# A planner's entry for four small products is changed from 110 to 225 each

## The chip, the cores and the metric

The kernel runs on one core of a Trainium2 chip. The metric is the device time of one execution in microseconds (us). Before the change it is 2021.24 us, the median of three runs (2019.19 to 2022.35). The profile that is quoted here comes from one execution of its own, which took 2021.44 us.

A core has five engines that run side by side, each in the order of its own program: PE (TensorE; its weight loads are listed apart, as PEld), DVE (VectorE), ACT (ScalarE), POOL (GpSimd) and SP (SyncE, which here issues most of the DMAs). PE writes its results to PSUM, which has eight banks.

## The reference

```python
x = A_x                                           # 2048 x 512, fp32
mod = (silu(c) @ w_mod).reshape(1, 6, 1, -1)
sa, ca, ga, sb, cb, gb = (mod[:, i] for i in range(6))
h = layernorm(x) * (1 + ca) + sa
x = x + ga * attention(h, A_wqkv, A_wo)           # 32 heads of 16, softmax over 2048 keys
h = layernorm(x) * (1 + cb) + sb
x = x + gb * mixer(h, B_w1, B_w2, B_w3, B_w4)     # shifts along the sequence, then an MLP of 1792
```

The attention is the long part: for each of 32 heads, 2048 x 2048 scores, their exponentials, and the product with V.

## The kernel before

**Stages.** A prologue makes the layer norm, the modulation rows and the first columns of Q, K and V. The attention follows, from about 100 to 1535 us of the span. The rest of Q, K and V is made between the products of the first units of the attention. A tail (the product with `wo`, the mixer, the MLP) ends the kernel.

**Units.** The attention runs over 64 units: 4 chunks of 512 queries, times 16 pairs of heads. A unit has 16 key tiles of 128 keys, and each key tile has two half rows, one for each head of the pair, so a unit has 32 half rows. For a half row, PE makes two products side by side on different rows of its array: `sc` (L1012), 512 scores of the present unit, and `mb` (L996), scores of a unit that is 24 key tiles ahead, from which only the maximum is wanted. DVE reduces `mb` to a maximum (`mx`, L992). ACT takes the exponential of `sc` (`pt`, L1008) into integers of 32 bits. Their upper halves are read as fp16 as they stand. The lower halves have to be converted first, one instruction for each key tile: the function `p_low` gives it to POOL (L1061), or to ACT when the planner's clock for POOL is more than 200 ahead of that for ACT (the profile lists those under L156, the planner's line that calls them). PE then adds up P V from the upper halves (`pv`, L1086) and the lower halves (L1083) in one PSUM bank that stays with the unit.

**Blocks.** PE's program is made of blocks: three half rows (six products into six different banks of the seven that go round), then the `pv` products that are due. A unit is 10 and two thirds blocks, so that the pattern repeats after three units and 32 blocks. Units are numbered from 0; unit u is of the first, second or third kind as u divided by 3 leaves 0, 1 or 2.

**The shift rows.** When all maxima of a unit are there, `max_fin` makes its row of shifts: a reduction on DVE (L1042), two small copies on ACT (L1043, L1044), a difference on POOL (L1045), and then eight small DMAs issued by SP (`qtl<-nm`), which write the shifts as extra rows into the Q tile `qtl`. The first `sc` product of that unit reads these rows.

**The end of a unit.** ACT copies the finished sums to SBUF (`ac`, L1103). The first `pv` product of the next unit overwrites the same bank and has to wait for that copy. Then `o_fin` (L1107) transposes the sums with four products, `ot` (L1113), into one of the seven banks. ACT copies the result out (`sm`, L1120), which frees that bank; DVE takes the reciprocals of the row sums (`rc`, L1128), and POOL writes the quotients (L1124).

**The planner.** No engine chooses an order on the chip. When the kernel is built, a class `Sched` keeps a clock for each engine. `put` (L154) adds the cost of an instruction to its engine's clock and emits it; everything is emitted in the order that these clocks give. Work like `o_fin` is a generator: after each product it yields its cost, and `one` (L213) takes that from a budget and adds it to PE's clock. `fill` (L234) runs generators at the end of a block, as far as the budget goes. `gap` (L203) runs them when PE's clock would have to wait 500 or more for a bank or for `pt`, until the wait is filled up to 60. PE's clock also sets when a chain of the other engines counts as ready, when `p_low` prefers ACT, and when a bank counts as free.

Of the kernel before, what the change touches and what calls it, by code (L numbers as in the profile page):

```python
# [330 lines left out]
def kernel(ctx, tc, A_x, A_wqkv, A_wo, B_w1, B_w2, B_w3, B_w4, c, w_mod, out):  # L331
# [23 lines left out]
    def mark(key):  # L355
        return None, 0, lambda: done.add(key)
# [68 lines left out]
    def dbank(n):  # L425
        return sch.take(lambda i: psd["d"].tile([P, CH], F32, name=n, tag=f"s{i}" if psd["s"] else f"d{i}", bufs=1))
# [669 lines left out]
    def ac_copy():  # L1096
        u, e = acs.pop()
        while u and ("ot", u - 1) not in done:
            sch.step()
        ac = at.tile([P, CH], F32, name="ac", tag="ac", bufs=1)  # L1100
        vst.pop(u)
        acc = pv.pop(u)
        e = sch.crit("A", cA(), e + PX, lambda: act.activation(ac, acc, AF.Copy))  # L1103
        v_free[0] = e + XP["A"]
        sch.add(o_fin(u, ac, e + XP["A"]), 0)

    def o_fin(u, ac, ready):  # L1107
        ci, pr = units[u]
        yield lambda: sch.T["P"] >= ready and sch.room()
        n = 2 * (DH + 1)  # L1110
        b = dbank("ot")[:, :TPC * n]
        for t in range(TPC):
            te.matmul(b[:, t * n:(t + 1) * n], ac[:, t * P:(t + 1) * P], smat.rearrange("p j d -> p (j d)"), start=True, stop=True)  # L1113
            yield 110
        done.add(("ot", u))
        sm = at.tile([P, 8, DH + 1], F32, name="sm", tag="sm", bufs=2)
        rc = at.tile([P, 8, 1], F32, name="rc", tag="rc", bufs=2)

        def sums():
            act.activation(sm.rearrange("p th d -> p (th d)"), b, AF.Copy)  # L1120
            sch.free(b)

        def fin():
            pool.tensor_tensor(osb[ci][:, :, pr * 32:pr * 32 + 32].rearrange("p t (h d) -> p t h d", d=DH),  # L1124
                              sm[:, :, 0:DH].rearrange("p (t h) d -> p t h d", h=2),
                              rc.rearrange("p (t h) o -> p t h o", h=2).to_broadcast([P, TPC, 2, DH]), op=OP.mult)

        sch.chain(("A", 170, sums), ("D", 90, lambda: dve.reciprocal(rc, sm[:, :, DH:DH + 1])), ("G", 350, fin),  # L1128
                  *([mark(("att", ci))] if pr == NP - 1 else []), prio=0, bank=b)
# [601 lines left out]
```

## Time and profile before

| | us |
|---|---|
| median of three runs | 2021.24 |
| the profiled execution | 2021.44 |
| its span, first to last instruction | 2019.7 |
| PE busy in the span | 1934.4 (96%) |
| DVE busy | 1656.3 (82%) |
| POOL busy | 1571.9 (78%) |
| ACT busy | 1510.2 (75%) |

The profiled execution lies 0.2 us above the median, and 1.7 us of it lie outside the span. From about 500 to 1490 us the attention runs with nothing between its products but the four products of each unit: there all four engines are above 90%.

### The profile page before, as it was taken

How to read it: one execution, taken by the hardware profiler on the slowest of the kernel's cores; microseconds unless marked ns; L12 is line 12 of the kernel's file. 1: busy time of each engine (PE TensorE's matmuls, PEld its weight loads, DVE VectorE, ACT ScalarE, POOL GpSimd, SP SyncE). 2: the span in 40 equal slices, each digit the busy share in tenths (PEclk: the TensorE clock that was granted, in tenths of full speed). 3: DMA queues.
4: the chain of work that ended last, by engine and by line, in shares of the span. 5: the costliest groups of instructions: out<-in, count | busy, mean ns of one | idle time of the engine just before them, and what ended most of it. 6: DMA issues, size and time to landing. Idle time of an engine off the chain costs nothing.

```text
span 2019.7 us, 41655 instructions
## 1 busy us (share of the span) xinstructions
PE 1934.4 (96%) x14456; PEld 1162.1 (58%) x14456; DVE 1656.3 (82%) x2979; ACT 1510.2 (75%) x3085; POOL 1571.9 (78%) x1488
## 2 busy tenths in 40 slices
PE   7999999999999999999999999999998999999999
PEld 5755545454444444444444444444455878898998
DVE  6398888879999999999999999999975886556443
ACT  6438987768999999999999999999985544344443
POOL 6349988879999999999999999999996554435222
PEclk9989999999999999999999999999999999999999
DMA  8777675445343434444443435354414676553541
GB/s 295 233 204 192 151 187 155 135 130 124 86 92 87 91 88 83 96 82 97 81 98 75 104 72 107 72 136 126 99 46 158 230 261 265 226 200 116 201 153 68
DMA packets 185508, 278.01 MB, mean 138 GB/s; under 512 B 117104, under 2 KB 127856, under 8 KB 169008
## 3 DMA queue, kind: packets, MB, share of 16 engines
q1 hardware_dynamic: 181792, 267.20, 49.1%
q10 hardware_dynamic: 2304, 4.20, 0.6%
q0 software_dynamic: 1200, 3.93, 0.5%
q8 instruction: 115, 1.88, 0.4%
q14 instruction: 97, 0.79, 0.1%
HBM read 211.81 MB, written 62.91 MB: 136 GB/s over the span
## 4 chain that ended last, share of the span: by engine, by line
PE 61%; DVE 16%; ACT 9%; issue 6%; POOL 4%; DMA 3%; SPq 0%; ACTq 0%; POOLq 0%; DVEq 0%
PE mb L996 13%; DVE mx L992 12%; PE pv L1086 9%; PE sc L1012 8%; ACT pt L1008 7%; PE w L363 5%; PE w L359 5%; PE w L361 5%; PE pv L1083 4%; PE ot L1113 3%; POOL pt L1061 2%; PE xT L1247 1%; POOL trs L1356 1%; PE v L359 1%; DMA wr<-Ws 1%
## 5 line engine op out<-in xcount | busy, mean ns | idle before, releaser
L1061 POOL TENSOR_SCALAR pt<-pt 128x1024 f16<-128x1024 uint16 x953 | 1248.3, 1367 | 79.9 <-ACT pt L1008 76.7
L992 DVE TENSOR_REDUCE mx<-mb 128x1 f32<-128x512 f32 x2048 | 1250.0, 681 | 72.7 <-PE mb L996 63.5
L1008 ACT ACTIVATE pt<-sc 128x512 int32<-128x512 f32 x2048 | 1060.9, 614 | 123.5 <-PE mb L996 97.1
L996 PE MATMUL mb<-kst,qtl 62*128 62x512 f32 x2048 | 781.1, 461 | 20.5 <-ACT pt L1008 10.0
L1012 PE MATMUL sc<-qtl,kst 64*128 64x512 f32 x2048 | 739.3, 449 | 4.6 <-DVE mx L992 1.8
L996 PEld LDWEIGHTS mb<-kst,qtl 62*128 62x128 f32 x2048 | 358.9, 193 | 233.7 <-ACT pt L1008 160.4
L1012 PEld LDWEIGHTS sc<-qtl,kst 64*128 64x128 f32 x2048 | 336.6, 185 | 185.4 <-DVE mx L992 118.7
L1086 PE MATMUL pv<-pt,vst 128*32 128x512 f16 x4096 | 384.8, 397 | 20.6 <-ACT ac L1103 20.6
L1460 POOL TENSOR_TENSOR g<-sq,g 128x256 fp32r<-128x256 f32 (+1 forms) x124 | 96.8, 785 | 188.9 <-ACT g L1459 176.6
L1083 PE MATMUL pv<-pt,vst 128*32 128x512 f16 (+1 forms) x2048 | 220.8, 389 | 2.5 <-POOL pt L1061 2.4
L1086 PEld LDWEIGHTS <-vst 128*32 128x32 bf16 x4096 | 91.8, 93 | 227.2 <-issue 208.8
L361 PE MATMUL w<-A,wr 128*128 128x256 f32 (+1 forms) x520 | 153.4, 295 | 0.3 <-DVE A L349 0.3
L359 PE MATMUL w<-A,wr 128*128 128x256 f32 (+1 forms) x520 | 153.2, 295 | 0.3 <-ACT A L353 0.3
L363 PE MATMUL w<-A,wr 128*128 128x256 f32 (+1 forms) x520 | 153.1, 294 | 0.0
L1456 ACT ACTIVATE sq<-w 128x256 f32<-128x256 f32 (+1 forms) x130 | 52.1, 401 | 127.0 <-PE w L363 117.5
L363 PE MATMUL w<-wr,g 128*128 128x512 f32 x270 | 106.5, 394 | 3.1 <-POOL g L1460 3.1
L359 PE MATMUL w<-wr,g 128*128 128x512 f32 x270 | 106.9, 396 | 1.8 <-DMA wr<-Ws 1.8
L361 PE MATMUL w<-wr,g 128*128 128x512 f32 x270 | 106.1, 393 | 0.0
L1438 DVE SCALAR_TENSOR_TENSOR sq<-sq,w 128x256 f32<-128x256 f32 (+1 forms) x130 | 58.1, 449 | 56.5 <-ACT sq L1458 56.3
L359 PEld LDWEIGHTS w<-A,wr 128*128 128x128 f32 x520 | 98.7, 190 | 1.7 <-ACT A L353 0.5
L361 PEld LDWEIGHTS w<-A,wr 128*128 128x128 f32 x520 | 98.7, 190 | 1.6 <-DVE A L349 0.5
L363 PEld LDWEIGHTS w<-A,wr 128*128 128x128 f32 x520 | 98.6, 190 | 0.5 <-issue 0.5
(156 smaller groups left out, 2131.6 us busy)
## 6 DMA issues: line engine op xcount, KB each, us to landing
wr<-Ws SPq DMA_DIRECT2D x66, 1024.0 KB, 5.2
vst<-Vs SPq DMA_DIRECT2D x64, 768.0 KB, 5.7
kst<-Ks SPq DMA_DIRECT2D x126, 384.0 KB, 6.1
Ws<-wr SPq DMA_DIRECT2D x14, 1024.0 KB, 5.0
qtl<-Qs SPq DMA_DIRECT2D x128, 96.0 KB, 4.3
Vs<-vt SPq DMA_DIRECT2D x32, 384.0 KB, 4.2
Ks<-qk SPq DMA_DIRECT2D x16, 512.0 KB, 3.8
Qs<-qk SPq DMA_DIRECT2D x16, 512.0 KB, 3.0
```

The costliest lines, as they stand in the source:

```text
L359: te.matmul(o, lh, rh, start=first, stop=False)
L361: te.matmul(o, lh, rl, start=False, stop=False)
L363: te.matmul(o, ll, rh, start=False, stop=last)
L992: end = sch.crit("D", 605, e + PX, lambda: dve.reduce_max(mxs[u][:, j, g, c:c + 1], b, axis=AX.X))
L996: return ready, lambda: te.matmul(b, lhs, kst[u % 3][r, c * CH:(c + 1) * CH], start=True, stop=True), after
L1008: ea = sch.crit("A", 480, e + PX, lambda: act.activation(pt[s][:, j], b, AF.Exp))
L1012: return ready, lambda: te.matmul(b, kst[u % 3][r, kt * P:(kt + 1) * P], qst[u][r], start=True, stop=True), after
L1061: e_low[s] = XP["G"] + sch.crit("G", 1345, ready, lambda: pool.tensor_scalar(o, i, 0.5, 1.0, op0=OP.mult, op1=OP.mult))
L1083: te.matmul(acc[r:r + n, :], v[:, kt + i, c:c + n].bitcast(F16), pt[s + i].bitcast(F16)[:, j, 0::2], start=False, stop=kt == NKT - 2, skip ...
L1086: te.matmul(acc[r:r + 32, :], v[:, kt, r:r + 32], pt[s].bitcast(F16)[:, j, 1::2], start=kt == 0, stop=False, skip_group_check=True)
L1113: te.matmul(b[:, t * n:(t + 1) * n], ac[:, t * P:(t + 1) * P], smat.rearrange("p j d -> p (j d)"), start=True, stop=True)
L1460: ("G", cG(n), lambda: pool.tensor_tensor(lo, sq, hi, op=OP.subtract)), (None, 0, end), bank=b)
```

## The change

One number is changed: what `o_fin` yields for each of the four `ot` products. The products stay the same. The kernel's instructions are the same too, but for 15 conversions of lower halves that go from ACT (71 before, 56 now) to POOL (953, now 968). What changes is their order, from unit 2 to the start of the tail.

```diff
         for t in range(TPC):
             te.matmul(b[:, t * n:(t + 1) * n], ac[:, t * P:(t + 1) * P], smat.rearrange("p j d -> p (j d)"), start=True, stop=True)
-            yield 110
+            yield 225
         done.add(("ot", u))
```

**ACT, around the start of unit 40.** In these rows `pt<-sc` are exponentials, `pt<-pt` is a conversion of lower halves, `mf` and `nm` are the two small copies of the shift rows of unit 40, `ac` is the copy of the sums of unit 39. The first exponential of unit 40 is the fifteenth of the 21 in the fourth row before, and the twelfth of the 18 in the sixth row now. Before:

```order
L1008 ACTIVATE pt<-sc 128x512 x3
L1043 ACTIVATE mf<-mf 128x8
L1044 ACTIVATE nm<-mf 128x8
L1008 ACTIVATE pt<-sc 128x512 x21
L156 ACTIVATE pt<-pt 128x1024
L1103 ACTIVATE ac<-pv 128x512
L1008 ACTIVATE pt<-sc 128x512 x6
L1120 ACTIVATE sm<-ot 128x136
```

The same stretch now:

```order
L1120 ACTIVATE sm<-ot 128x136
L1008 ACTIVATE pt<-sc 128x512 x6
L156 ACTIVATE pt<-pt 128x1024
L1043 ACTIVATE mf<-mf 128x8
L1044 ACTIVATE nm<-mf 128x8
L1008 ACTIVATE pt<-sc 128x512 x18
L1103 ACTIVATE ac<-pv 128x512
L1008 ACTIVATE pt<-sc 128x512 x9
```

The conversion that stood right ahead of `ac` has gone from there, and one stands right ahead of the shift rows, which have moved three exponentials back. The first happens in 13 units more than it is undone (17 copies `ac` stood right behind a conversion, 4 do now); the second in 13 units of the second kind (19, 22, 25, 28, 37 and every third to 61). In units 16, 31 and 34 the shift rows stand as late, without a conversion ahead of them.

**PE, the products of unit 38.** Before, at the end of a block (`pv`), with the next block (`mb`, `sc`) behind them:

```order
L1086 LDWEIGHTS vst
L1086 MATMUL pv<-pt,vst 32x512
L1113 MATMUL ot<-smat,ac 128x34 x4
L996 MATMUL mb<-kst_967,qtl_965 128x512
L1012 MATMUL sc<-qtl_145,kst_147 128x512 x2
```

Now three of the four stand at that place, and the fourth at the end of the block after the next:

```order
L1083 LDWEIGHTS vst
L1083 MATMUL pv<-pt,vst 32x512
L1113 MATMUL ot<-smat,ac 128x34
L996 MATMUL mb<-kst_967,qtl_965 128x512
L1012 MATMUL sc<-qtl_145,kst_147 128x512 x2
```

39 of the 64 units are split in two like this, where one was before. The copy `sm` on ACT stands up to six exponentials later than before, so the bank of `ot` stays taken for two blocks more.

**ACT, the end of the attention.** Before, the last exponentials are followed by work of the tail (`sq`) and the last `ac`:

```order
L1008 ACTIVATE pt<-sc 128x512 x8
L1456 ACTIVATE sq<-w_24626 128x256
L1456 ACTIVATE sq<-w_24672 128x256
L1458 ACTIVATE sq<-sq 128x256 x2
L1103 ACTIVATE ac<-pv 128x512
```

Now the very last conversion is ACT's, and 36 products of the tail that PE ran before the last `ot` (three `w` groups of `A` and `wr`) follow it:

```order
L1008 ACTIVATE pt<-sc 128x512 x2
L156 ACTIVATE pt<-pt 128x1024
L1367 ACTIVATE xn<-xb,trs 128x512
L1103 ACTIVATE ac<-pv 128x512
L1120 ACTIVATE sm<-ot 128x136
L1456 ACTIVATE sq<-w_24670 128x256
```

The copy `ac` and the last `sm` now stand ahead of the tail's `sq`.

## The prediction

> **What bounds the kernel now.** I read the page first, its engines and the table of waits, then the windows, then the timeline of one period of three units, engine by engine.
>
> ```profile
> span 2019.7 us, 41655 instructions
> PE 1934.4 (96%) x14456; PEld 1162.1 (58%) x14456; DVE 1656.3 (82%) x2979; ACT 1510.2 (75%) x3085; POOL 1571.9 (78%) x1488
> ...
> core 0: us, PE busy (x) PEld busy (x) DVE busy (x) ACT busy (x) POOL busy (x), PEclk, DMA share, GB/s
> 900.00:1000.00 100.00, 96.32 (x826) 45.84 (x830) 95.47 (x166) 91.80 (x182) 95.83 (x82) 1.00 0.44 91
> 1500.00:1600.00 100.00, 88.37 (x548) 66.69 (x545) 67.17 (x133) 55.20 (x113) 64.95 (x83) 0.97 0.45 159
> ```
>
> The windows tell more than the shares of the whole span. From 900 to 1000 us, in the middle of the attention, PE, DVE and POOL are each busy for some 96 us of 100, and ACT for 92. No engine is free, and none is full. The chain of waits gives the length of the pattern: the same group of three exponentials comes up once in three units.
>
> ```profile
> 896.98 1.30 ACT pt L1008 x3
> 957.99 1.30 ACT pt L1008 x3
> ```
>
> That is 61.01 us for three units, 20.34 for one. The next rows, of the timeline, give what DVE and POOL need for a unit when they run without a gap.
>
> ```profile
> 902.21 10.85 DVE L992 TENSOR_REDUCE mx<-mb 128x1 f32<-128x512 f32 x18 [0.42 <-PE mb L996]
> 900.47 11.64 POOL L1061 TENSOR_SCALAR pt<-pt 128x1024 f16<-128x1024 uint16 x9
> 940.69 0.40 POOL L1124 TENSOR_TENSOR osb<-sm,rc 128x128 f32<-128x128 f32 x1
> 919.96 0.20 POOL L1045 TENSOR_TENSOR nm<-mf,nm 128x8 fp32r<-128x8 f32 x1
> ```
>
> DVE: 32 maxima at 10.85/18 = 0.603 us are 19.3, with two small reductions of about 0.1 each 19.5. POOL: 16 conversions less the 4 in three units that ACT takes are 14.67, at 11.64/9 = 1.293 us 19.0, with 0.40 and 0.20 19.6. Both are under 20.34, so each engine loses 0.7 to 0.8 us a unit in waits for the others. The waits from 500 to 1490 us:
>
> ```profile
> PEld mb L996 <- ACT pt L1008: 142.4, 417, 0.8
> ...
> POOL pt L1061 <- ACT pt L1008: 31.9, 45, 1.2
> DVE mx L992 <- PE mb L996: 27.2, 59, 0.8
> ...
> PE pv L1086 <- ACT ac L1103: 18.7, 16, 1.2
> ```
>
> PE waits for ACT to free banks, DVE for PE, POOL for ACT: a ring that is held together by seven banks, in which a delay on one engine reaches the others when it is longer than what is queued. So the price of the change is that of the long single delays that it adds and takes away.
>
> **What the change takes away: `ac` behind a conversion.** ACT, DVE and PE in the timeline, at the end of a unit of the first kind:
>
> ```profile
> 910.59 1.36 ACT L156 ACTIVATE pt<-pt 128x1024 f16<-128x1024 uint16 x1
> 911.79 0.60 ACT L1103 ACTIVATE ac<-pv 128x512 f32<-128x512 f32 x1
> ...
> 912.44 0.63 PE L1086 MATMUL pv<-pt,vst 128*32 128x512 f16 x8 [1.17 <-ACT ac L1103]
> ...
> 913.80 1.89 DVE L992 TENSOR_REDUCE mx<-mb 128x1 f32<-128x512 f32 x3 [0.73 <-PE mb L996]
> 916.22 1.89 DVE L992 TENSOR_REDUCE mx<-mb 128x1 f32<-128x512 f32 x3 [0.54 <-PE mb L996]
> ```
>
> The conversion holds ACT for 911.79 - 910.59 = 1.20 us, `ac` comes that much later, PE stands still for 1.17, and DVE then has gaps of 0.73 and 0.54: the delay goes through whole. The table above has 16 of these waits, 18.7/16 = 1.17 each. With 17 such places before and 4 now, 13 x 1.17 = 15.2 us of PE's waiting go.
>
> **What it adds: late shift rows.** In the second kind of unit they now come three exponentials later and behind a conversion. Before, such a unit looks like this (DVE's last reduction, ACT's second copy, SP's DMAs, and the pair of `sc` whose second is the first of the new unit):
>
> ```profile
> 898.03 0.18 DVE L1042 TENSOR_REDUCE mf<-mx 128x8 f32<-128x32 f32 x1
> 898.69 0.21 ACT L1044 ACTIVATE nm<-mf 128x8 fp32r<-128x8 f32 x1
> 898.93 5.28 SPq L135 DMA_DIRECT2D qtl<-nm  x8
> 905.45 0.61 PE L1012 MATMUL sc<-qtl,kst 64*128 64x512 f32 x2
> ```
>
> The first `sc` is wanted some 0.2 us after the pair's start, about 905.65, 7.6 us after the reduction began. One unit of before, unit 13, has its shift rows as late as the changed plan has them, without the conversion (the third row is a piece of the chain of waits, the fourth is PEld's):
>
> ```profile
> 470.21 0.17 DVE L1042 TENSOR_REDUCE mf<-mx 128x8 f32<-128x32 f32 x1
> 471.77 0.21 ACT L1044 ACTIVATE nm<-mf 128x8 fp32r<-128x8 f32 x1
> 476.38 2.00 DMA qtl<-nm
> 478.49 0.22 PEld L1012 LDWEIGHTS sc<-qtl,kst 64*128 64x128 f32 x2 [0.50 <-DVE mx L992]
> ...
> 479.02 1.57 ACT L1008 ACTIVATE pt<-sc 128x512 int32<-128x512 f32 x3 [0.30 <-PE sc L1012]
> 470.31 14.43 DVE L992 TENSOR_REDUCE mx<-mb 128x1 f32<-128x512 f32 x24
> ```
>
> The last of the eight DMAs lands at 478.38, 6.61 us after ACT's copy began and 8.2 after the reduction. PE's load stood 0.50 us, ACT 0.30, and DVE not at all: 24 maxima in 14.43 us are 0.60 each. So 0.50 is about the slack. With a conversion of 1.20 us ahead of the copies, PE stands 0.50 + 1.20 = 1.7 us at the first `sc`, and the `mb` and `pv` behind it stand with it. Of the 1.7, between nothing (`ac`'s rows, where all went through) and 0.5 (unit 13) is absorbed; I take the middle, 1.45, as there is no reason for either end. 13 units x 1.45 = 18.9 us, ends 15.6 and 22.1. Units 16, 31 and 34 are like unit 13 and cost nothing, 1.5 at most. POOL's part of the shift rows isn't late, since the conversion ahead of it is the one that ACT took.
>
> **The bank that is held longer.** For 39 split units one of seven banks is missing for two more blocks. DVE's gaps behind PE are 27.2/59 = 0.46 us each. One gap more in each split unit would be 18 us; none, 0. I take one in four, 4 us, nearer to nothing, because the blocks still find six free banks for six products.
>
> **The split product.** One more change of weights per split unit on PE, against a shorter burst:
>
> ```profile
> 936.95 0.97 PEld L1113 LDWEIGHTS ot<-smat,ac 128*128 128x128 f32 x8 [0.24 <-DVE mx L992]
> 936.95 1.08 PE L1113 MATMUL ot<-smat,ac 128*128 128x34 f32 x8
> ```
>
> The four products (eight passes) take 1.08 us, so the fourth takes 0.27. If it falls wholly into a wait, 39 x 0.27 = 10.5 us are gained; if the 0.24 of lead-in is paid again, 39 x 0.24 = 9.4 are lost. I take 0: PEld's waits for banks (142.4/417 = 0.34 each) are there to cover it, and there is no row for more.
>
> **Conversions from ACT to POOL.** 15 x 1.293 = 19.4 us more on POOL, covered by its 31.9 us of waiting for ACT; 15 x 1.20 = 18 us less on ACT, which is off the path but where it delays `ac` or the shift rows, and that is counted above. Cost 0; without the cover, the third rival.
>
> **Both ends of the attention.** In the first 14 units the higher entry takes 14 x 4 x 115 ns = 6.4 us of the planner's budget from the products of Q, K and V, which so come later; they are needed only before unit 16, and PE has the same work. I take 0, with 3 us either way. At the other end POOL sets the pace, and PE's last wait is for it:
>
> ```profile
> 1524.48 2.60 POOL pt L1061 x2
> ...
> 1527.12 0.41 PE L1083 MATMUL pv<-pt,vst 128*32 128x512 f16 x3 [0.62 <-POOL pt L1061]
> ```
>
> One conversion fewer there is 2.60/2 = 1.3 us gained. The 36 products of the tail behind the last `ot` cost 0, as PE runs without a gap on either side of it; if DVE or ACT were late for them, 36 x 0.12 = 4.3 (the starts at 1528.26, 1528.38 in the next row show the step).
>
> ```profile
> 1528.26 0.28 PE L359 MATMUL w<-A,wr 128*128 128x256 f32 x1
> 1528.38 0.27 PE L361 MATMUL w<-A,wr 128*128 128x256 f32 x1
> ```
>
> **The sum.** -15.2 + 18.9 + 4 - 1.3 = +6.4 us. On the profiled execution's 2021.4 us (0.2 above the median) that is 2028.
>
> **Rivals.** *Faster.* The shift rows' delay is absorbed, as DVE's queue was not touched in unit 13, and the removed waits stand alone. It decides below (15.2 + 1.3 - 4)/13 = 0.96 us of loss in each late unit. For it speaks that a longer gap on DVE was often made up by the ring:
>
> ```profile
> 975.74 0.20 DVE L1128 RECIPROCAL rc<-sm 128x8 f32<-128x8 f32 x1 [1.68 <-ACT sm L1120]
> ...
> 975.95 3.57 DVE mx L992 x6
> 979.72 17.88 DVE mx L992 x30
> ```
>
> DVE lost 1.68 us here, and then 36 maxima ran with next to no gap (the last two rows are pieces of the chain). At 0.2 us a unit the time is 2021.4 - 16.5 + 4 + 2.6 = 2011.5. Against it: a stop of PE in the middle of a block stops every other engine. *No change.* The two delays are of one size, and the bank costs nothing: 2021. *POOL becomes the bound.* With 15 conversions a unit it needs 15 x 1.293 + 0.60 = 20.0 us; if it still waits as now, 31.9 us over 990/20.34 = 48.7 units or 0.66 each, a unit takes 20.66, 0.32 more, over 48.7 units 15 us on top of the 6: 2043. Against it: most of its waits come from ACT's conversions, of which there are fewer.
>
> A fourth: POOL's added conversions hold up DVE. If every one of the 15 stopped a maximum for its 1.293 us, 19.4 us would come on top: 2047. The row of 18 maxima above speaks against it, since DVE kept 0.603 us a maximum beside POOL's nine conversions back to back. The Trainium skill, Perfetto Trace Analysis, Optimizing Scalar/DVE Operations, warns that these two engines share a read port, so that moving work between them may not help. By that rule the fourth rival would hold; the trace does not bear it out for maxima that are read from PSUM.
>
> **How the numbers follow.** A measurement of this kernel can tell some 0.2% (4 us) from no change. The forecast has 0.41, the faster rival 0.30, no change 0.17, POOL as the bound 0.10, the fourth 0.02. Slower together is 0.53. The ends of the terms above (15.6 to 22.1, 0 to 18, -10.5 to 9.4, 3 either way) do not all fall together; the forecast's own range is 2025 to 2038. The range for all is 2009 to 2046: from a little below the faster rival to beyond POOL's.
>
> **What would show it.** Right: a row "PE sc L1012 <- DMA qtl<-nm" of about 13 waits of 1 to 2 us; "PE pv L1086 <- ACT ac" down to 2 or 3 waits; the period of three units near 61.4 us; 56 conversions on ACT. Wrong: waits for these DMAs below 1 us each, a period under 60.7, or POOL busy for 99 us of 100 with DVE's maxima still 0.60. The forecast fails most easily in what the ring absorbs, for which two rows speak differently.

## The result, and the profile after

Five runs of the kernel after have a median of 2029.59 us (2028.39 to 2032.29), five of the kernel before 2019.84 us (2018.74 to 2022.35). The ratio is 1.0050, with a 95% interval of 1.0036 to 1.0064: some 10 us slower. The forecast was 2028. The number is right, and that is luck in good part: most of its terms are wrong in size and one is missing, as the experiments show.

The profiled execution of the kernel after is the longest of its five, 2.7 us above the median. Its page, and two windows of its trace (busy us of each engine, with the number of instructions):

```profile
span 2030.5 us, 41688 instructions
PE 1956.6 (96%) x14456; PEld 1178.6 (58%) x14456; DVE 1663.7 (82%) x2979; ACT 1492.3 (73%) x3070; POOL 1589.5 (78%) x1503
...
core 0: us, PE busy (x) PEld busy (x) DVE busy (x) ACT busy (x) POOL busy (x), PEclk, DMA share, GB/s
900.00:1000.00 100.00, 98.47 (x818) 47.34 (x814) 95.68 (x167) 89.16 (x181) 97.04 (x84) 1.00 0.43 90
1500.00:1600.00 100.00, 86.71 (x541) 62.86 (x541) 60.79 (x121) 57.44 (x118) 62.95 (x79) 0.95 0.36 127
```

ACT has 15 instructions fewer and POOL 15 more, the conversions that moved. The period of three units, in the chain of waits of the kernel after:

```profile
1182.70 1.11 ACT pt L1008 x3
1244.37 1.09 ACT pt L1008 x3
```

It is 61.67 us, against 61.01 before. The waits from 500 to 1490 us (us in total, times, longest; the first row says that DVE's `mx` waited for PE's `mb`) show what took the place of the 16 waits for `ac`:

```profile
DVE mx L992 <- PE mb L996: 32.9, 93, 1.8
...
ACT mf L1043 <- DVE mf L1042: 11.1, 24, 0.6
...
PE sc L1012 <- DMA qtl<-nm: 7.4, 10, 2.1
...
PEld mb L996 <- ACT sm L1120: 5.3, 13, 2.7
...
PE pv L1086 <- ACT ac L1103: 3.0, 4, 1.2
```

Three rows are new or nearly so. PE waits for the DMAs of the shift rows, 10 times (nine waits of 0.50 to 0.70 us and one of 2.13); PE's loads wait for `sm`, that is, for the bank of `ot`; and ACT waits 24 times for VectorE's last reduction of a unit. The prediction did not see this last one. Its row in the table of the kernel before:

```profile
ACT mf L1043 <- DVE mf L1042: 0.2, 1, 0.2
```

The timeline of the kernel after shows both kinds of unit. First a unit of the second kind, with late shift rows (the reduction on VectorE, a conversion and the first of the two copies on ACT, SP's DMAs, the pair of score products and the first exponentials of the new unit):

```profile
1141.14 0.18 DVE L1042 TENSOR_REDUCE mf<-mx 128x8 f32<-128x32 f32 x1
1142.49 1.39 ACT L156 ACTIVATE pt<-pt 128x1024 f16<-128x1024 uint16 x1
1143.71 0.21 ACT L1043 ACTIVATE mf<-mf 128x8 f32<-128x8 f32 x1
...
1144.19 4.98 SPq L135 DMA_DIRECT2D qtl<-nm  x8
1150.76 0.49 PE L1012 MATMUL sc<-qtl,kst 64*128 64x512 f32 x2 [0.64 <-DVE mx L992]
1151.26 1.09 ACT L1008 ACTIVATE pt<-sc 128x512 int32<-128x512 f32 x2 [0.71 <-PE sc L1012]
```

The copies start 2.57 us after the reduction, and ACT stands 0.71 us before the first exponentials. Now the other kind, where the copies come right behind the reduction:

```profile
1158.69 1.88 DVE L992 TENSOR_REDUCE mx<-mb 128x1 f32<-128x512 f32 x3 [0.24 <-PE mb L996]
1160.68 0.18 DVE L1042 TENSOR_REDUCE mf<-mx 128x8 f32<-128x32 f32 x1
...
1160.90 0.21 ACT L1043 ACTIVATE mf<-mf 128x8 f32<-128x8 f32 x1 [0.60 <-DVE mf L1042]
```

VectorE does three maxima before the reduction, and ACT, which takes its instructions in order, stands 0.60 us in front of a copy of 0.21, with exponentials behind it. The Trainium skill, PSUM — Partial Sum Buffer, Engine vs sequencer instructions, says that the queues of ScalarE, VectorE and GpSimd are strictly first in, first out; this row agrees.

Where the time goes along the span is read from the copies `ac`, one for each unit. Those of units 12, 27, 54 and 57, in the timeline of the kernel after:

```profile
478.54 0.63 ACT L1103 ACTIVATE ac<-pv 128x512 f32<-128x512 f32 x1
...
784.69 0.61 ACT L1103 ACTIVATE ac<-pv 128x512 f32<-128x512 f32 x1
...
1339.50 0.62 ACT L1103 ACTIVATE ac<-pv 128x512 f32<-128x512 f32 x1
...
1408.07 0.62 ACT L1103 ACTIVATE ac<-pv 128x512 f32<-128x512 f32 x1
```

and of the kernel before:

```profile
483.42 0.60 ACT L1103 ACTIVATE ac<-pv 128x512 f32<-128x512 f32 x1
...
789.58 0.59 ACT L1103 ACTIVATE ac<-pv 128x512 f32<-128x512 f32 x1
...
1339.23 0.60 ACT L1103 ACTIVATE ac<-pv 128x512 f32<-128x512 f32 x1
...
1400.99 0.60 ACT L1103 ACTIVATE ac<-pv 128x512 f32<-128x512 f32 x1
```

The kernel after is 4.9 us ahead at unit 12 and still at unit 27, 0.3 behind at unit 54, 7.1 behind at unit 57 and 7.9 behind at unit 60. The span ends 10.8 us later. So it loses 5.2 us over nine periods, then 6.8 in a single one, from unit 54 to 57, and some 3 from unit 60 to the end.

The single period has two stops of PE, of 2.37 and 2.13 us, that no term of the prediction describes. The rows of the first stop, and the one row of the second:

```profile
1366.67 2.44 ACTq L1281 DMA_DIRECT2D x<-in_A_x_dram  x2
1369.16 0.28 ACT L1120 ACTIVATE sm<-ot 128x136 f32<-128x136 f32 x1 [2.32 <-issue]
1369.49 0.79 PE L996 MATMUL mb<-kst,qtl 62*128 62x512 f32 x1 [2.37 <-ACT sm L1120]
...
1403.08 0.54 PE L1012 MATMUL sc<-qtl,kst 64*128 64x512 f32 x2 [2.13 <-DMA qtl<-nm]
```

In every kernel here ACT issues four loads of the tail (`x`, L1281) just ahead of this `sm`. In the profiled execution of the kernel after one of these issues took 1.95 us, so that `sm` came late and PE stood for the bank of `ot`. In the profiles of the six kernels without the change none took more than 0.45; in five of the other seven with it one took 0.65 to 1.39. Why is open. In the kernel before, the same place holds ACT for 0.99 us, and PE does not wait for it:

```profile
1362.77 1.41 ACTq L1281 DMA_DIRECT2D x<-in_A_x_dram  x3
...
1364.23 0.29 ACT L1120 ACTIVATE sm<-ot 128x136 f32<-128x136 f32 x1 [0.99 <-PE ot L1113]
```

From 1370 to 1380 us, behind the first stop, the granted clock of PE (the third number from the end) is 0.69 in the kernel after and 1.00 before:

```profile
1370.00:1380.00 10.00, 10.00 (x74) 3.86 (x72) 7.43 (x13) 8.18 (x16) 7.21 (x8) 0.69 0.19 48
```

```profile
1370.00:1380.00 10.00, 9.90 (x84) 4.21 (x82) 9.82 (x17) 9.30 (x18) 9.40 (x8) 1.00 0.56 105
```

(The first row is of the kernel after.) From 1400 to 1410 us it is 0.83, against 1.00. No run shows whether the other four executions have these stops, nor what the lower clock is worth by itself. The period takes 61.8 us in the kernel before and 68.6 in the kernel after.

### The profile page after: what moved, and what is told of

The parts are those of the page before. It is cut to its first block, busy times and chain, and to the rows that moved or that the text cites. A ratio compares the mean times of both kernels' runs of the same rounds, so it can differ in the third digit from the quotient of the medians.

```text
span 2030.5 us, 41688 instructions
## 1 busy us (share of the span) xinstructions
PE 1956.6 (96%) x14456; PEld 1178.6 (58%) x14456; DVE 1663.7 (82%) x2979; ACT 1492.3 (73%) x3070; POOL 1589.5 (78%) x1503
## 4 chain that ended last, share of the span: by engine, by line
PE 62%; ACT 7%; DVE 6%; issue 4%; POOL 3%; DMA 3%; SPq 2%; ACTq 0%; POOLq 0%; DVEq 0%
PE mb L996 15%; PE sc L1012 11%; PE pv L1086 10%; PE w L359 5%; PE w L363 5%; PE w L361 5%; ACT pt L1008 5%; PE pv L1083 4%; PE ot L1113 3%; DVE mx L992 3%; SPq L135 2%; DMA qtl<-nm 1%; ACT pt L156 1%; POOL trs L1356 1%; PE xT L1247 1%
## 5 line engine op out<-in xcount | busy, mean ns | idle before, releaser
L1061 POOL TENSOR_SCALAR pt<-pt 128x1024 f16<-128x1024 uint16 x968 | 1267.1, 1368 | 72.4 <-ACT pt L1008 71.3
L996 PE MATMUL mb<-kst,qtl 62*128 62x512 f32 x2048 | 790.0, 464 | 16.9 <-ACT pt L1008 5.2
```

What stands on the lines that cost most here:

```text
L996: return ready, lambda: te.matmul(b, lhs, kst[u % 3][r, c * CH:(c + 1) * CH], start=True, stop=True), after
L1061: e_low[s] = XP["G"] + sch.crit("G", 1345, ready, lambda: pool.tensor_scalar(o, i, 0.5, 1.0, op0=OP.mult, op1=OP.mult))
```

## The experiments

Twelve kernels, all with five rounds against the kernel before. The first four were to tell the prediction's terms apart; the rest came from what they showed. The difference is the ratio less one, times 2020 us. An interval is some 2 to 3 us either way, so a difference between two rows of the table carries some 3 to 4 us either way.

| kernel | ratio | 95% interval | against before |
|---|---|---|---|
| after | 1.0050 | 1.0036 to 1.0064 | +10.1 us |
| a_early: after, copies behind the reduction in every unit | 1.0106 | 1.0093 to 1.0119 | +21.4 |
| b_late3: before, shift rows three exponentials later in 15 units | 1.0005 | 0.9995 to 1.0016 | +1.0 |
| b_acfirst: before, `ac` ahead of the conversion | 0.9997 | 0.9988 to 1.0007 | -0.6 |
| a_unsplit: after, the four products together | 1.0130 | 1.0117 to 1.0143 | +26.3 |
| a_hold02: after, copies of two kinds two exponentials later | 1.0016 | 1.0006 to 1.0025 | +3.2 |
| a_place1: after, copies of the second kind two exponentials earlier | 1.0012 | 1.0002 to 1.0022 | +2.4 |
| a_place: after, both of these | 0.9981 | 0.9971 to 0.9991 | -3.8 |
| b_early2: before, copies of two kinds one exponential behind the reduction | 1.0018 | 1.0007 to 1.0028 | +3.6 |
| b_late4: before, shift rows four exponentials later | 1.0051 | 1.0037 to 1.0065 | +10.3 |
| a_place_unsplit: a_place, the four products together | 1.0023 | 1.0013 to 1.0032 | +4.6 |
| a_place_split: a_place, the second kind split too | 1.0009 | 0.9999 to 1.0018 | +1.8 |
| b_early02: before, copies of two kinds right behind the reduction | 1.0095 | 1.0078 to 1.0112 | +19.2 |

All of them keep the planner's clocks as they are and change only the place at which single instructions are written. Where lines are added, the line numbers in the rows move: the copy `mf` is L1043 in the kernel before and up to L1059 in these.

### `ac` ahead of the conversion, in the kernel before (b_acfirst)

```diff
-                e_low[s] = XP["A"] + sch.crit("A", CLOW, ready, partial(act.activation, o[:, c], i[:, c], AF.Copy, scale=0.5))
+                e_low[s] = XP["A"] + sch.crit("A", CLOW, ready, lambda: sch.conv.append(
+                    (s, partial(act.activation, o, i, AF.Copy, scale=0.5))))
...
+        conv = sch.conv[:]
+        sch.conv.clear()
         e = sch.crit("A", cA(), e + PX, lambda: act.activation(ac, acc, AF.Copy))
+        for _, fn in conv:
+            fn()
```

> The kernel before, with each of the 17 conversions that ACT runs right ahead of the copy of a unit's sums (ac, L1103) put right behind that copy; all 71 conversions stay on ACT, and no other engine's order changes. Theory A (each collision costs PE the 1.17 us that it waits in pv for ac): 17 x 1.17 = 19.9 us less, 2000 us. Theory B (the wait is a place where PE waits for other work that is late anyway): 2017 to 2020 us, with PE's waits for ac gone and those for VectorE or the exponentials longer by as much.

-0.6 us (-2.4 to +1.4): theory B. A new row among the waits from 500 to 1490 us in this kernel:

```profile
PE pv L1093 <- ACT pt L1117: 6.5, 16, 0.4
```

The 18.7 us of waits for `ac` are gone, and 16 new ones of 0.4 us stand at the product that needs the delayed conversion. So some 12 us of these waits have gone on balance, and the time has not moved. PE's 1.17 us at `ac` were not on the path, at least not the 0.77 of them that went, although VectorE had gaps of 0.73 and 0.54 behind them.

### The shift rows late, in the kernel before (b_late3, b_late4)

```diff
             ea = sch.crit("A", 480, e + PX, lambda: act.activation(pt[s][:, j], b, AF.Exp))
+            if sch.held:
+                sch.wait_exps += 1
+                if sch.wait_exps >= 3:
+                    for fn in sch.held:
+                        fn()
...
+        def held(fn):
+            late = u % 3 == 1 and 19 <= u <= 61
+            return (lambda: sch.held.append(fn) if u not in sch.gone else fn()) if late else fn
         sch.chain(("D", 85, lambda: dve.reduce_max(mf.rearrange("p (j g) -> p j g", j=2), mx, axis=AX.X)),
-                  ("A", 100, lambda: act.activation(mf, mf, AF.Copy, scale=-1.0, bias=PEXP)),
+                  ("A", 100, held(lambda: act.activation(mf, mf, AF.Copy, scale=-1.0, bias=PEXP))),
...
```

> The kernel before, with ACT's two copies of the shift rows, and so POOL's difference and the eight DMAs, held until three further exponentials have been written, in the 15 units 19, 22, ... 61 alone: 11 instead of 14 exponentials ahead of the unit's start, the place that they have after the change. Nothing else moves on any engine. Theory A: each of the 15 units makes PE stand at its first score product, 15 x 1.45 = 21.8 us, 2041.6 us. Theory B (another wait of PE gives the lateness back within the unit): 2020 to 2024 us, with the waits for the DMA there and the waits for VectorE's maxima shorter.

+1.0 us (-1.0 to +3.2): the time of theory B. Over units 20 to 53 the copies of the second kind begin a median of 1.81 us after the reduction instead of 0.37. The waits for the DMA that both theories expected hardly came: two, 0.8 us in all. The second kernel holds them by four exponentials (the 3 in the diff becomes a 4), 2.29 us after the reduction:

> The kernel before, with the two copies of the shift rows, POOL's difference and the DMAs held back by four exponentials in the 15 units 19, 22, ... 61, one more than in the run that held them by three (there the copies began 1.81 us behind VectorE's reduction instead of 0.37, PE waited 0.8 us in all for the DMA between 500 and 1490, and the time rose by 0.05%). Theory E (lateness is free until the rows land behind the first score product, then each 0.1 us costs 0.1 us): the copies move from 1.81 to about 2.3 us, PE waits some 0.4 us in each unit, 15 x 0.4 = 6 us, 2025 to 2029 us. Theory F (lateness is absorbed whatever its size, the loss of the change has another cause): 2018 to 2022 us.

+10.3 us: another half microsecond of lateness costs some 9 us more (6 to 13) in 15 units. This speaks for theory E, with a higher price, but the table of waits, here of the kernel held by three and below of that held by four, shows two waits that grew:

```profile
POOL nm L1057 <- ACT nm L1056: 1.3, 5, 0.4
PE sc L1021 <- DMA qtl<-nm: 0.8, 2, 0.4
```

```profile
POOL nm L1057 <- ACT nm L1056: 9.9, 22, 0.6
...
PE sc L1021 <- DMA qtl<-nm: 1.9, 4, 0.7
```

POOL's order was left as it was, so POOL stood some 0.55 us for the late copies in each of the 15 units, and PE's wait for the DMA alone is too small for 9 us. The two parts are not told apart by this run. The two tables also come from executions of 2027.88 and 2025.99 us, which stand the other way round than the medians (2021.76 and 2030.65), so they show which waits there are, not what these cost. The times show that in these 15 units copies some 1.8 us behind the reduction cost nothing that can be told from the noise, and copies 2.3 us behind it do. The kernel after has a median of 2.60.

### The copies right behind the reduction, in the kernel after (a_early)

```diff
-        sch.chain(("D", 85, lambda: dve.reduce_max(mf.rearrange("p (j g) -> p j g", j=2), mx, axis=AX.X)),
-                  ("A", 100, lambda: act.activation(mf, mf, AF.Copy, scale=-1.0, bias=PEXP)),
-                  ("A", 100, lambda: act.activation(nm[:, 0], mf, AF.Copy)),
+        def reduce_copy():
+            dve.reduce_max(mf.rearrange("p (j g) -> p j g", j=2), mx, axis=AX.X)
+            act.activation(mf, mf, AF.Copy, scale=-1.0, bias=PEXP)
+            act.activation(nm[:, 0], mf, AF.Copy)
+        sch.chain(("D", 85, reduce_copy), ("A", 100, lambda: None), ("A", 100, lambda: None),
...
```

> The kernel after, with ACT's two copies of the shift rows (L1043, L1044) written right behind VectorE's reduction in every unit, 14 to 16 exponentials ahead of the unit's start; 15 conversions still moved to POOL, the sums still split. Theory A (the late shift rows cost what the prediction gave them, 18.9 us): 2029.6 - 18.9 = 2010.7 us, faster than before by 9 us, and the waits of the first score product for the DMA of the shift rows (10 of 2.1 us between 500 and 1490) vanish. Theory B (the loss lies in the sums: split products, banks held longer): 2027 to 2031 us, the waits for the DMA vanish and the time moves into other waits of PE.

Neither: 11 us slower than the kernel after. (The expectation misreads the table: the 10 waits for the DMA are 7.4 us in all, and 2.1 is the longest.) These waits vanished as expected, and two other rows grew:

```profile
ACT mf L1044 <- DVE mf L1043: 24.7, 47, 0.9
...
PE mb L996 <- ACT sm L1122: 13.6, 12, 3.8
```

ACT now stands for the reduction in nearly every unit, 13.6 us more than in the kernel after, and PE stands for `sm`, which ACT reaches late. This miss led to theory C: some of the loss of the change is ACT's standing for the reduction in the units whose copies the change brought up to it.

### The two places of the copies apart, in the kernel after (a_hold02, a_place1, a_place)

The first kernel holds the copies of the first and third kind back by two exponentials (23, 26, 29, 30, 33 and 63 stay), the second writes those of the second kind two exponentials earlier, the third does both. `flush_held` writes what is held when the given number of exponentials has passed. The diff is that of the third; in the first the two conditions `u % 3 == 1 and u >= 16` are false, and in the second `late` is:

```diff
+            sch.flush_held(2 if u % 3 else max(2 - 1, 0), u + 1)
...
+        def reduce():
+            dve.reduce_max(mf.rearrange("p (j g) -> p j g", j=2), mx, axis=AX.X)
+            if u % 3 == 1 and u >= 16:
+                sch.held += [copy1, copy2]
...
+        def held(fn):
+            if u % 3 == 1 and u >= 16:
+                return (lambda: None) if fn in (copy1, copy2) else fn
+            late = u % 3 != 1 and u >= 14 and u not in (23, 26, 29, 30, 33, 63)
+            return (lambda: sch.held.append(fn) if u not in sch.gone else fn()) if late else fn
+        sch.chain(("D", 85, reduce), ("A", 100, held(copy1)), ("A", 100, held(copy2)),
+                  ("G", 250, held(diff)), (None, 0, held(shift_rows)), mark(("shift", u)), prio=0, ready=sch.T["D"])
```

> The kernel after, with ACT's two copies of the shift rows (and with them POOL's difference and the DMAs) written two exponentials later in the units from 14 on whose copies the change had brought up to VectorE's reduction (of each three units the two that are not the second kind; six single units excepted); the second kind stays late, only ACT's order changes. Theory C (new: the change costs what ACT, which runs in order, stands in front of the copies until the reduction is done, 24 waits and 11.1 us between 500 and 1490 against 0.2 us before): the waits vanish, 2019 to 2023 us. Theory D (the late shift rows of the second kind, and the banks): 2028 to 2031 us.

> The kernel after, with the two copies written two exponentials earlier (13 instead of 11 ahead of the unit's start) in the second kind of unit alone, units 16 to 61; the other two kinds stay right behind the reduction, only ACT's order changes. Theory C (ACT's standing for the reduction is the loss): no change, 2028 to 2031 us. Theory D (late shift rows): the waits of the first score product for the DMA vanish, 7.4 us in 10 waits between 500 and 1490, and 2020 to 2023 us.

> Both edits: the kernel after, with the copies of the second kind two exponentials earlier and those of the other two kinds two exponentials later. Theory C and theory D both take part: if each is worth what it waits, 2029.6 - 11.1 - 7.4 = 2011 us, faster than the kernel before; if only C holds, 2019 to 2023 us.

The first is 6.9 us faster than the kernel after (1.0050 - 1.0016 = 0.34%), the second 7.7, each some 3.5 either way, and both together 13.9, close to their sum of 14.6. In the tables of waits the first has no row for the reduction and keeps that of the DMA, the second the reverse. Their rows, of the first and of the second:

```profile
PE sc L1023 <- DMA qtl<-nm: 5.7, 10, 0.9
```

```profile
ACT mf L1059 <- DVE mf L1054: 11.1, 24, 0.6
```

So both theories hold, each for a part: ACT's standing costs 6.9 us (11.1 us of waits), the late shift rows 7.7 (7.4 us of waits). In the traces some of both gains lies in one place: the period from unit 54 to 57 takes 68.6 us in the kernel after, 64.1 in the first, 61.9 in the second and in the third. With both removed, only 0.3 us of either wait is left:

```profile
PE sc L1023 <- DMA qtl<-nm: 0.3, 1, 0.3
```

This kernel is the fastest of all: 0.19% under the kernel before (0.09 to 0.29%).

### The copies behind the reduction, in the kernel before (b_early2, b_early02)

The same cause, put into the kernel before. The first attempt gave the copies of the first and third kind to ACT at the next exponential:

```diff
...
+            if u % 3 != 1 and u >= 14:
+                sch.held += [copy1, copy2]
...
```

> The kernel before, with the two copies written right behind VectorE's reduction in the 34 units from 14 on that are not of the second kind, the place that the change gives them; nothing else moves. Theory C: ACT stands some 0.3 to 0.6 us in each, 34 x 0.45 = 15 us, and the time rises by about as much (writing them there in all units of the kernel after added 13.6 us of these waits and 13 us): 2030 to 2036 us. Theory D: 2018 to 2022 us.

+3.6 us, between the two theories, but it was no test: the copies landed mostly 0.2 to 1.0 us behind the reduction, and its table has no row in which ACT waits for it. What it has is a wait of PE's loads for the copy itself, where there was none before:

```profile
PEld mb L1006 <- ACT mf L1059: 6.2, 14, 0.5
```

The second attempt wrote them one exponential earlier, in the same units (`early`):

```diff
         def reduce():
             dve.reduce_max(mf.rearrange("p (j g) -> p j g", j=2), mx, axis=AX.X)
+            if early:
+                copies()
...
```

> The kernel before, with the two copies written on ACT directly behind the place of VectorE's reduction in the units from 14 on that are not of the second kind, one exponential earlier than in the run that moved them to two ahead and made no waits; nothing else moves. Theory C: ACT stands for the reduction as in the kernel after, some 11 to 15 us between 500 and 1490 in 24 to 33 waits, and the time is 5 to 10 us above the kernel before, 2025 to 2030 us. Rival: the kernel before has room for these waits, 2018 to 2022 us.

+19.2 us (15.8 to 22.6): theory C, with a price above its range.

```profile
DVE mx L992 <- PE mb L996: 42.9, 104, 0.8
...
ACT mf L1045 <- DVE mf L1049: 17.5, 32, 0.9
...
PE mb L996 <- ACT pt L1008: 15.0, 31, 0.6
```

ACT stood 17.5 us. PE then waited 15.0 us for exponentials (7.9 before), and VectorE 42.9 us for PE (27.2 before): VectorE's waits for PE grew by 15.7 us, nearly as much as ACT stood. One exponential decides between 3.6 and 19.2 us.

### The four products together, or three and one (a_unsplit, a_place_unsplit, a_place_split)

In the kernel after, all four where the first stood:

```diff
         for t in range(TPC):
             te.matmul(b[:, t * n:(t + 1) * n], ac[:, t * P:(t + 1) * P], smat.rearrange("p j d -> p (j d)"), start=True, stop=True)
+        for t in range(TPC):
             yield 225
```

> The kernel after, with the four transposing products of a block of a unit's sums (ot, L1113) written together where the first of them stood, so no longer two or three now and the rest a fill later; only TensorE's order changes, the plan's clocks stay. Theory A (the split is worth nothing): 2028 to 2031 us. Theory B (the split is a cost: TensorE's gaps ahead of ot rose from 5.9 to 19.0 us between 500 and 1490, that is some 13 us): 2015 to 2022 us, with those gaps back near 6 us. Theory C (the split helps, since fewer products stand between two score products): 2033 to 2040 us.

Theory C of that run: 16.2 us slower than the kernel after (1.0130 - 1.0050), beyond its range. Theory B read the gaps ahead of `ot` as a cost; they went back to 4.5 us as it expected, and the kernel got slower, since other waits grew more:

```profile
ACT pt L1008 <- PE mb L996: 70.8, 146, 1.5
DVE mx L992 <- PE mb L996: 44.6, 113, 1.4
```

VectorE waited 44.6 us for PE, against 32.9. Not all of the 16.2 need be waits: the four executions of this kernel have a granted clock of 0.986 to 0.988, the five of the kernel after 0.991 or 0.992. Among the 35 executions of the kernel before that were taken beside `a_place`, 0.001 less of clock goes with some 1.3 us more, so that by this estimate some 6 us go with the clock. Why it is lower here was not tested. The same edit on the fastest kernel, and a third kernel in which the second kind is split as well (its fourth product and `sm` half a block later):

> The kernel after with both edits on the copies (second kind two exponentials earlier, the others two later), and the four transposing products of a block together where the first stood. Theory G (the split itself saves what writing them together cost in the kernel after, 17.9 us): 2015.4 + 17.9 = 2033 us. Theory H (that cost came through the copies that stood wrongly): 2013 to 2019 us.

> The kernel after with both edits on the copies, and the fourth transposing product also of the second kind of unit (16 to 58, 15 units, of which those not yet split gain it) written half a block later, so that every kind is split into three and one. Theory G (a split saves some 17.9 us / 35 split units = 0.5 us each): about 10 units x 0.5 = 5 us less, 2010 us. Theory H: 2013 to 2018 us.

Together costs 8.4 us there (1.0023 - 0.9981; 5.6 to 11), half of what it cost in the kernel after: between the two theories. To split the second kind too costs 5.6 us (1.0009 - 0.9981; 3 to 8), against both. PE's waits for the bank of `ot` grew with it, from 3.7 and 0.8 us to:

```profile
PEld mb L1013 <- ACT sm L1168: 8.9, 15, 2.1
...
PE mb L1013 <- ACT sm L1168: 5.3, 5, 1.8
```

A reading of this that the waits allow, and no run shows by itself: a split saves a longer stop of the score products and pays with a bank that is held longer, and which is more differs from place to place.

## Why the prediction was right, and where it was not

- **The step that failed first is the gain: `ac` behind a conversion, -15.2.** Taking away all 17 of these waits in the kernel before gave 0.6 us (-1.4 to 2.4), though 6.5 us of waiting came back for the delayed conversions; 13 of them would give 0.5. In the kernel after the waits went as forecast, 18.7 us in 16 to 3.0 in 4, but "the delay goes through whole" was wrong. Two gaps of VectorE behind the wait were taken for the loss, without looking whether the next period began later.
- **The late shift rows, +18.9: the mechanism was right, the size was not.** Moving them back gained 7.7 us. 1.7 us of standing in 13 units were predicted; between 500 and 1490 us nine waits of 0.50 to 0.70 were seen, and the one of 2.13. What made them late was as forecast (copies 2.57 us after the reduction, behind a conversion). The 1.7 was built on the 0.50 of unit 13, taken as what the lateness costs without the conversion; `b_late3` shows that three exponentials of it cost nothing that can be told from the noise. That other waits of the ring move the first score product back as well is likely, but not shown.
- **A step was missing: the other two kinds of unit.** The same change of ACT's order that made one kind late brought the copies of the other two up to the reduction. The prediction followed the late ones only. ACT's standing there cost 6.9 us by the run that held them back.
- **The split product, 0 (between -10.5 and +9.4).** The split saves 8.4 us once the copies stand well, near the end of gain. The reason given for 0, that the loads' mean wait of 0.34 us covers it, did not hold.
- **The bank held longer, +4.** Its waits appear: 5.3 us in 13 waits of PE's loads, where the whole kernel before has one of 0.2. But 2.7 of them are one wait, the stop at 1369 us, which came of ACT's DMA issues. A longer hold in the second kind cost 5.6 us net. The change's own share was not measured.
- **The first 14 units, 0 with 3 either way.** At unit 12 the eight kernels with the change stand at a mean of 479.5 us, the six without it at 482.3, each kind within 3 us of its mean: 2.7 us gained, within the bounds.
- **The end of the attention, -1.3 and 0 for the 36 products.** From the copy `ac` of unit 60 to PE's last `pv` the kernel before takes 71.8 us and the kernel after 68.9; from there to the end of the span 485.9 and 491.8. So more than the 1.3 was gained, but the 36 products were not free behind it: 3.0 us are lost on balance in this profile, 0.9 in that of `a_hold02` and 1.4 in that of `a_place1`. These are single executions.
- **The rivals *faster* and *no change*.** Both took the removed waits for a gain of 15 us, and fell with it. What the first said of the shift rows, that the ring makes up for much, holds up to 1.8 us of lateness in `b_late3`; it holds for `ac` as well.
- **Conversions to POOL, 0, and the two rivals on POOL.** The fastest kernel has these 15 conversions on POOL, so they do not make it the bound. VectorE's maxima took 681 ns in the mean before and 679 after, with 15 more conversions beside them, so the fourth rival falls. The prediction drew it from the shared read port. What the Trainium skill, Perfetto Trace Analysis, Optimizing Scalar/DVE Operations, says is that GpSimd and VectorE share an SBUF read port. The maxima are read from PSUM, so these two means neither bear that out nor speak against it, and no other run here does.

```profile
L992 DVE TENSOR_REDUCE mx<-mb 128x1 f32<-128x512 f32 x2048 | 1250.0, 681 | 72.7 <-PE mb L996 63.5 <-PE sc L1012 5.4
```

```profile
L992 DVE TENSOR_REDUCE mx<-mb 128x1 f32<-128x512 f32 x2048 | 1258.2, 679 | 74.3 <-PE mb L996 64.2 <-PE sc L1012 4.7
```

(The first row is of the kernel before, the second of the kernel after; busy us, mean ns, then VectorE's idle time ahead of them.)

The measured terms are -0.5 + 7.7 + 6.9 - 8.4 - 2.7 = +3.0, and the result is +10.1. Most of these terms carry some 3 us either way. The 7.1 us that are left stay open: the end of the attention has 1 to 3 of them by the profiles, the banks may have some, and the terms act on each other (together instead of split cost 16.2 us with the copies wrong and 8.4 with them right, part of which goes with the clock). So +6.4 was forecast from terms of -15.2 and +18.9, both too large in size, and with an omission; that their errors nearly cancel is luck. Of the signs named beforehand, the waits for `ac` (4, not 2 or 3), the 56 conversions and the period (61.67, not 61.4) came nearly as said. The waits for the DMA came in number (10 of about 13) but not in length: nine of ten are below 1 us, which was named as a sign of being wrong. None of the signs could tell that the gain at `ac` was worth nothing.

## What to carry to other kernels

In a ring of engines that are all busy for some 90 us of 100 or more, a wait in the table is a place, not a price. Taking it away tells the price, and here it was 0.6 us for 18.7 us of one wait (6.5 of which came back elsewhere) and 6.9 us for 11.1 us of another. When a change moves instructions on an engine that takes them in order, look at those that come earlier as closely as at those that come later: one that comes before its input is ready stops all behind it. Here one exponential between a reduction and the small copy that needs it was the difference between 19.2 and 3.6 us. And follow the loss along the span before giving it to a term: here 6.8 us of the profiled execution's loss lay in one period, with two stops that come once in it.

## What the runs showed that was not expected

PE's busy time is no measure of its work here. From 500 to 1490 us the kernel before and the one with `ac` first have the same number of instructions on PE within 0.1% and the same time, but 12 us of difference in busy time:

```profile
500.00:1490.00 990.00, 958.74 (x8164) 455.01 (x8157) 949.09 (x1651) 915.32 (x1813) 948.45 (x808) 1.00 0.43 92
```

```profile
500.00:1490.00 990.00, 970.84 (x8173) 457.02 (x8173) 950.50 (x1654) 916.45 (x1816) 951.14 (x810) 1.00 0.43 92
```

(The first row is of the kernel before, the second of the one with `ac` first.) PE's waiting turned into longer products in the profile, where the ends of products are modelled. VectorE's maxima keep their length (681, 679 and 680 ns in the mean before, after and in the fastest kernel), so its busy time in the window follows the pace: 949.1 before, 943.9 after, 936.2 with the products together, 953.1 in the fastest kernel.
